# Retention attention and a multiplicative feed-forward: queries loaded four tokens to a partition, in tiles of four heads

## The chip, the core and the metric

The kernel runs on one core of a Trainium2 chip. Five engines work side by side on their own instruction queues: TensorE (PE, matrix products; PEld are its weight loads), VectorE (DVE), ScalarE (ACT), GpSimd (POOL) and SyncE (SP), whose queue here does nothing but issue DMA transfers. Sixteen DMA engines carry the transfers. The metric is the device time of the whole kernel in microseconds (us), smaller is better. Before the change it is 183.44 us, the median of three runs (183.2 to 184.47).

## The reference

There are 4 batches, 8 heads, 768 tokens and 64 elements a head. For each batch and head a 64 x 64 state runs through the tokens, and its output feeds a feed-forward network with three products:

```
gamma = 1.0 - 2.0 ** (-5.0 - np.arange(H))
state = gamma * state + outer(k[t], v[t])        # per batch and head
y[t]  = q[t] @ state / sqrt(64)
x = y.transpose(0, 2, 1, 3).reshape(3072, 512)   # tokens x (heads x 64)
out = ((x @ w1) * (x @ w2)) @ w3 @ w_out         # d_ff = 1024
```

Inputs and output are float32.

## The kernel before

**Tiling.** The recurrence is done in chunks: within a chunk of 128 tokens (two halves of 64) as masked products, between chunks through a state. A step m handles one chunk of two batches: steps 0 to 5 are the six chunks of batches 0 and 1, steps 6 to 11 those of batches 2 and 3. Only steps 0 and 1 are different: `Pairs` (L397) takes 256 tokens of one batch each. The products W3 x W_out are formed once at the start (`w3_transpose`, `w3_part`, `W3Block`), so that the feed-forward of a step is: `ab(f)` for eight blocks f (two products of 128 x 256, a copy by ScalarE, a multiplication by VectorE; L630 to L651), and `o_unit(e)` for two batches (eight products of 128 x 512, a copy, a store; L653).

**Attention of a step.** Four groups of 32 small matmuls (64 x 64 quarters of the array): `scores` (L375, k against q into `psA`), `intra` (L522, masked scores against v into `psY`), `kv` (L538, k against v into `psK`; 16 matmuls only in steps 5 and 11, the last chunks), and `inter` (L591, the state `t` against q, added to `psY`). `outputs_back` (L607) multiplies `psY` by the decays `YS` and writes the tokens of `XT` in their natural order. `ended` (L585) puts a tiny copy, the mark, on ScalarE after the last matmul of `intra`, and `inter` waits for it.

**Where q comes from.** `load_q(n)` (L71) loads tile n, 256 tokens (two chunks) of one batch and all eight heads, through `load_pairs` (L79): two neighbouring tokens stand on a partition, so that a contiguous run in memory is 2 x 64 floats, 512 bytes. `q_cast` (L280) turns the tile into float16 on GpSimd and puts the token's parity t outside the heads. The tile is then transposed in blocks of 128 columns: by TensorE for n = 0 to 3 (`q_transposes`, L318), by a DMA that transposes for n = 4 to 11 (`q_dma`, L336). After that each partition holds a head's element, with even tokens and odd tokens in two runs. `queries` (L368) picks the 64 columns of a half chunk: 2 runs of 32. The order of the columns, even tokens before odd ones, is known to three other places: the masks (`keep`, `keep_t`, L175), the exponents of the decays (`if_i`, L153) and `outputs_back`. k and v of steps 2 to 11 are loaded token by token (256 bytes a run, L93).

**Order of the work.** Nothing is planned by the compiler; the lines from L688 are the order on every engine. All loads, DMA transposes and most stores go through SyncE's queue in the order of the program. At the beginning this is: weights W3 and W_out, tiles of steps 0 and 1, W1, W2, then q 2, q 3, k 2, v 2, k 3, q 4, q 5, v 3, k 4, v 4. In a step m: the DMA transpose of k of step m + 1, the stores of step m - 2, one q tile, k and v of step m + 2, and in even steps the DMA transposes of two q tiles. `step(m)` (L880) starts with `intra(m - 1)`, `kv(m)`, `scores(m)` and `inter(m - 1)` one behind the other. For the steps in `EARLY` (L876), `intra(m - 1)` is instead issued in the step before, after two of the eight `ab` blocks, and `inter` needs no mark.

```
last = None if m in EARLY else ended(intra(m - 1))
...
inter(m - 1, last)
...
if m + 1 in EARLY:
    intra(m)
```

Of the kernel before, what the change touches and what calls it, by code (L numbers as in the profile page):

```python
# [12 lines left out]
MULT = mybir.AluOpType.mult  # L13
# [5 lines left out]
def kernel(  # L19
# [11 lines left out]
    nc = tc.nc  # L31
    B, H, S, D = q.shape
    C = 128
    L = 64
    WST = 22
    NCH = S // C
# [22 lines left out]
    def half(x):  # L59
        return slice(x * L, (x + 1) * L)  # L60

    def dma_in(dst, src):
        nc.sync.dma_start(dst, src)  # L63
# [5 lines left out]
    q_in, k_in, v_in = {}, {}, {}  # L69

    def load_q(n):  # L71

        g, e = divmod(n, 2)
        if g >= NSTEP // 2:
            return
        bp, cp = divmod(g, NCH // 2)
        q_in[n] = load_pairs(q, bp * 2 + e, cp)

    def load_pairs(src, b, cp):  # L79
        t = new_stage()  # L80
        dma_in(
            t[:, :].rearrange("p (h x) -> p h x", x=2 * D),
            src[b, :, cp * 2 * C : (cp + 1) * 2 * C, :].rearrange("h (p t) d -> p h (t d)", t=2),
        )
        return t
# [19 lines left out]
    def new_stage():  # L105
        return wstage.tile([128, 1024], FP, tag="wst", name="stg")
# [18 lines left out]
    for f in range(4, 8):  # L125
        w3_st.append(load_rows(moe_w3, f))
    for e in range(2):
        load_q(e)
        k_in[e] = load_pairs(k, e, 0)
        v_in[e] = load_pairs(v, e, 0)  # L130
    w1_st = [load_rows(moe_w1, d) for d in range(4)]
# [19 lines left out]
    for s in range(2):  # L151
        nc.gpsimd.iota(ip_i[half(s), 0:2, :], pattern=[[1, 2], [0, H]], base=1, channel_multiplier=2)
    if_i = const.tile([128, 2, L], mybir.dt.int32, name="if_i")  # L153
    nc.gpsimd.iota(if_i[:, :, :], pattern=[[L, 2], [1, 2], [2, 32]], base=1, channel_multiplier=0)
    LGH = const.tile([128, H], FP, name="LGH")
    LGP = const.tile([128, 2, NP], FP, name="LGP")
    for h in range(H):
# [2 lines left out]
    YS = const.tile([128, 3, NP, L], FP, name="YS")  # L160
# [12 lines left out]
    def masks_and_decays():  # L173

        nc.gpsimd.memset(keep[:, :], 1.0)  # L175
        for s in range(2):
            r = slice(s * L, (s + 1) * L)
            nc.gpsimd.affine_select(
                out=keep[r, :], in_=keep[r, :], compare_op=mybir.AluOpType.is_ge, fill=0.0,
                base=0, pattern=[[1, 2], [2, 32]], channel_multiplier=-1,  # L180
            )

        nc.gpsimd.memset(keep_t[:, :, :], 1.0)
        for s in range(2):
            for t in range(2):
                nc.gpsimd.affine_select(
                    out=keep_t[half(s), t, :], in_=keep_t[half(s), t, :], compare_op=mybir.AluOpType.is_ge,
                    fill=0.0, base=-t, pattern=[[1, 2], [2, 64]], channel_multiplier=-2,
                )
        for h in range(H):  # L190
            for s in range(2):
                nc.gpsimd.memset(LGP[half((h + s) % 2), s, h // 2 : h // 2 + 1], math.log(gam[h]))
        for h in range(H):
            p, r = h // 2, (h % 2) * 64
            nc.gpsimd.memset(GS[r : r + 64, p : p + 1], gam[h] ** C)
# [11 lines left out]
    XT = {}  # L207
# [70 lines left out]
    q16s, k16s, v16s, qTs, kTs, AMs, psYs, Ts = {}, {}, {}, {}, {}, {}, {}, {}  # L278

    def q_cast(n, *engs):  # L280
        if n not in q_in:
            return
        q16s[n] = att.tile([128, 1024], HP, tag="q16", name="q16", bufs=2)
        pairs_cast(q16s[n], q_in.pop(n), *engs)

    def pairs_cast(dst, src, *engs):
        n = H // len(engs)
        for i, eng in enumerate(engs):
            hs = slice(i * n, i * n + n)
            (nc.scalar.copy if eng is nc.scalar else eng.tensor_copy)(  # L290
                dst[:, :].rearrange("i (t h d) -> i h t d", t=2, d=D)[:, hs, :, :],
                src[:, :].rearrange("i (h t d) -> i h t d", t=2, d=D)[:, hs, :, :],
            )

    def k_cast(m, engs):
        k16 = att.tile([128, 2, 512], HP, tag="k16", name="k16", bufs=3)
        k32 = k_in.pop(m)
        if len(engs) == 1:
            parts = [(k16[:, :, :].rearrange("p e x -> p (e x)"), k32[:, :, :].rearrange("p e x -> p (e x)"))]
        else:  # L300
            parts = [(k16[:, e, :], k32[:, e, :]) for e in range(2)]
        for eng, (dst, src) in zip(engs, parts):
            (nc.scalar.copy if eng is nc.scalar else eng.tensor_copy)(dst, src)  # L303
        k16s[m] = k16
# [61 lines left out]
        )  # L366

    def queries(m, e, p, s, r):  # L368
        c = m % NCH
        i0 = c % 2 * 64 + s * 32  # L370
        return qTs[m // 2 * 2 + e][half(r), :, p, i0 : i0 + 32]

# [24 lines left out]
    class Pairs:  # L397
# [4 lines left out]

        def k_cast(self, *engs):
            self.k16 = att.tile([128, 1024], HP, tag="k16", name="k16", bufs=3)
            pairs_cast(self.k16, k_in.pop(self.e), *engs)

        def k_transposes(self, tag, on_dve, parts=1):
            self.kT = att.tile([128, 2, NP, 128], HP, tag="kT", name="kT", bufs=2)
# [9 lines left out]
            )  # L418

        def queries(self, r, p, s):  # L420
            return qTs[self.e][half(r), :, p, half(s)]

        def scores(self, t):
            am = att.tile([128, 2, NP, 128], HP, tag="am", name="am")
# [18 lines left out]
        def intra(self, t):  # L443
            if t == 0:
                self.y = [bank(f"Y{s}", [128, NP, 128], FP, "psY") for s in range(2)]
            for p in range(NP):
                for s in range(2):
                    for r in range(2):
                        c0 = p * 128 + r * 64
                        last = nc.tensor.matmul(  # L450
                            self.y[s][half(r), p, :], lhsT=self.v16[half(s), t, c0 : c0 + 64],
                            rhs=self.am[t][half(s), r, p, :], start=(t == 0 and p == 0),
                            stop=(s == 0 and t == 1 and p == NP - 1),
                        )
            return last
# [50 lines left out]
        def outputs_back(self, s):  # L506
            if self.e not in XT:
                XT[self.e] = xpool.tile([128, NP * 2, 2, L], HP, tag="xt", name="xt")
            nc.vector.tensor_tensor(
                XT[self.e][:, :, :, :].rearrange("p (a s) b x -> p a s (b x)", s=2)[:, :, s, :]  # L510
                .rearrange("p a (b i t) -> p a t b i", b=2, t=2),
                self.y[s][:, :, :].rearrange("p a (t b i) -> p a t b i", t=2, b=2),
                YS[:, 0:2, :, :].rearrange("p b a (t i) -> p a t b i", t=2), MULT,
            )


# [68 lines left out]
    def ended(mm, eng=None):  # L585

        mark = (eng.tensor_copy if eng else nc.scalar.copy)(mark_t[:, :], Z[0:1, 0:1])
        wait_for(mark, mm)
        return mark
# [17 lines left out]
    def outputs_back(m, s):  # L607
        if m not in XT:
            XT[m] = xpool.tile([128, NP * 2, 2, L], HP, tag="xt", name="xt")
        swap = s == 1 and m % NCH > 0  # L610
        for to in (half(0), half(1)) if swap else (slice(0, 128),):
            fr = half(1 - to.start // L) if swap else to
            n = fr.stop - fr.start
            nc.vector.tensor_tensor(  # L614
                XT[m][to, :, s, :].rearrange("p (a e) (i t) -> p a e t i", e=2, t=2),
                psYs[m][s][fr, :, :].rearrange("p (a e) (t i) -> p a e t i", e=2, t=2),
                YS[fr, s + swap, :, :].unsqueeze(2).broadcast_to((n, NP, 2, L))
                .rearrange("p a e (t i) -> p a e t i", t=2),
                MULT,
            )  # L620

# [106 lines left out]
    wb.mm(4)  # L728
    wb.back()
    q_cast(0, nc.gpsimd)  # L730
    wb = W3Block(5)
    wb.mm(4)
# [117 lines left out]
    def step2():  # L850
        am_back = scores(2)
        am_back(0)
        am_back(1)
        stores.append(f0.o_unit(1, store=False))
        k_cast(3, (nc.gpsimd, nc.scalar))
        for n in (4, 5):
            q_cast(n, nc.gpsimd)
        for n in (4, 5):
            q_dma(n)
        for store in stores:  # L860
            store()
        for f in range(2, 5):
            f1.ab(f)
        intra(2)
        kv_back = kv(2, True)
        kv_back(0)
        f1.ab(5)
        k_transposes(3, None)
        f1.ab(6)
        kv_back(1)  # L870
        v_cast(3, (nc.gpsimd, nc.gpsimd))
        f1.ab(7)

    EARLY = (6, 11, 12)  # L876

    K_PE = (3, 5)

    def step(m):  # L880

        kv_backs = []
        if m > 4:
            last = None if m in EARLY else ended(intra(m - 1))
            if m < NSTEP:
# [27 lines left out]
        for f in range(2):  # L913
            ffn[m - 1].ab(f)
        if m + 1 in EARLY:
            intra(m)
# [61 lines left out]
```

## Time and profile before

| what | value |
|---|---|
| time, median of 3 | 183.44 us |
| profiled span | 181.5 us |
| TensorE busy | 175.3 us (97%) |
| VectorE, ScalarE, GpSimd busy | 108.6, 71.9, 71.3 us |
| DMA packets | 79,531, of which 57,361 under 512 B |
| DMA moved | 39.71 MB, mean 219 GB/s |
| q loads | 12 of 512 KB, 6.4 us from issue to landing (median) |
| k and v loads of steps 2 to 11 | 40 of 256 KB, 5.6 us |
| DMA transposes of q, of k | 8 and 6, 4.9 and 4.6 us |
| granted TensorE clock | 0.999 |

The page of a profile gives busy times, then the span in 40 slices (a digit is a busy share in tenths), the DMA queues, the chain of work that ended last, the costliest groups, and the DMA issues. A line of a timeline is: start, duration, engine, line of the kernel, operation, what is written <- what is read, shapes, and how often; in square brackets stands how long the engine was idle before, and who ended that. A line of the chain in order of time has start, duration and the work. Reading of a row by stretch: from and to, its length, busy time of each engine with the number of instructions, the granted clock, the share of the DMA engines and GB/s.

### The profile page before, as it was taken

What the parts mean: (1) busy time and instruction counts of PE and PEld (TensorE: products, weight loads), DVE (VectorE), ACT (ScalarE), POOL (GpSimd) and SP (SyncE); (2) the same over time, 40 slices, a digit from 0 to 9 for tenths busy, and PEclk for the clock granted to TensorE, in tenths of its full rate; (3) what the DMA queues carried; (4) which work ended last, traced back from release to release, by engine and by line L of the source; (5) the groups of instructions that cost most, each with busy time, mean ns of one, the idle gap of its engine ahead of it and who ended that gap; (6) DMA issues with size and microseconds to landing.
All of it is one profiled execution on the core that took longest, in us unless ns stands there. A gap on an engine that the chain in (4) does not pass through costs nothing.

```text
span 181.5 us, 6220 instructions
## 1 busy us (share of the span) xinstructions
PE 175.3 (97%) x2634; PEld 125.4 (69%) x2634; DVE 108.6 (60%) x204; ACT 71.9 (40%) x156; POOL 71.3 (39%) x127
## 2 busy tenths in 40 slices
PE   7889999999999999999999999999999999999992
PEld 2445656688766785876967858768688587685871
DVE  1246658751769669558477584494674956745430
ACT  3354845555631341524334424244243332442431
POOL 3127536964537752725427273055460350000000
PEclk9999999999999999999999999999999999999999
DMA  5999999999999999999999999999999940201203
GB/s 204 376 417 401 298 291 350 409 371 242 194 256 226 182 301 211 203 312 198 245 202 198 295 169 244 190 208 265 236 114 261 178 149 4 116 0 42 78 0 116
DMA packets 79531, 39.71 MB, mean 219 GB/s; under 512 B 57361, under 2 KB 74001, under 8 KB 79505
## 3 DMA queue, kind: packets, MB, share of 16 engines
q1 hardware_dynamic: 79072, 38.81, 88.6%
q8 instruction: 20, 0.33, 0.8%
q10 hardware_dynamic: 432, 0.52, 0.8%
q14 instruction: 7, 0.05, 0.1%
HBM read 29.36 MB, written 6.29 MB: 196 GB/s over the span
## 4 chain that ended last, share of the span: by engine, by line
PE 88%; DMA 5%; ACT 2%; SPq 1%; DVE 1%; issue 0%; ACTq 0%
PE psF L636 41%; PE psO L663 23%; DMA stg<-in_moe_w_out_dram 5%; PE psF L795 4%; PE psW L269 3%; PE psW L255 3%; PE psY L531 2%; PE psY L599 2%; PE psA L383 2%; PE psG L636 2%; PE psK L551 2%; PE psTq L328 1%; PE psW L244 1%; SPq L63 1%; PE psTk L357 1%; PE psY L450 1%
## 5 line engine op out<-in xcount | busy, mean ns | idle before, releaser
L636 PE MATMUL psF<-xt,w 128*128 128x256 f16 x672 | 76.7, 273 | 0.0
L636 PEld LDWEIGHTS <-w 128*128 128x128 f16 x704 | 68.4, 98 | 10.3
L651 DVE TENSOR_TENSOR ht<-pa,psF 128x256 f16<-128x256 f32 x88 | 36.9, 420 | 37.6 <-PE psF L636 32.0
L645 ACT COPY pa<-psF 128x256 f32<-128x256 f32 x80 | 29.8, 373 | 37.5 <-PE psF L636 37.5
L663 PE MATMUL psO<-w3o,ht 128*128 128x512 f16 (+2 forms) x200 | 43.9, 371 | 0.0
L667 ACT ACTIVATE osb<-psO 128x512 f32<-128x512 f32 (+2 forms) x25 | 14.5, 581 | 44.0 <-PE psO L663 44.0
L663 PEld LDWEIGHTS <-ht 128*128 128x128 f16 x200 | 18.5, 98 | 19.4
L614 DVE TENSOR_TENSOR xt<-psY,YS 64x512 f16<-64x512 f32 (+1 forms) x29 | 21.1, 727 | 4.8 <-PE psY L599 4.4
L310 POOL TENSOR_TENSOR v<-stg,VS 128x512 f16<-128x512 f32 x20 | 20.6, 1042 | 5.4 <-DMA stg<-in_v_dram 5.4
L303 POOL CAST k<-stg 128x512 f16<-128x512 f32 x18 | 11.0, 612 | 26.1 <-DMA stg<-in_k_dram 25.9
L290 POOL CAST q<-stg 128x1024 f16<-128x1024 f32 (+1 forms) x12 | 12.0, 1003 | 17.9 <-DMA stg<-in_q_dram 13.8
L390 DVE TENSOR_TENSOR am<-psA,keep 128x512 f16<-128x512 f32 x20 | 12.8, 682 | 0.6 <-PE psA L383 0.6
L566 POOL TENSOR_TENSOR t<-s,GS 128x512 f16<-128x512 f32 x8 | 8.3, 1039 | 7.8 <-DVE s L565 7.8
L248 DVE COPY w3t<-psW 128x1024 f16<-128x1024 f16 x8 | 5.5, 690 | 5.3 <-PE psW L244 5.3
L269 PE MATMUL psW<-wo,w3t 128*128 128x512 f16 x32 | 8.6, 381 | 0.0
L255 PE MATMUL psW<-wo,w3t 128*128 128x512 f16 x32 | 8.0, 387 | 0.7 <-ACT wo L224 0.5
L795 PE MATMUL psF<-xt,w 128*128 128x256 f16 x64 | 8.3, 273 | 0.2
L686 PE MATMUL psZ<-zeros 128*128 128x512 f16 (+1 forms) x18 | 6.6, 504 | 1.3 <-DVE zeros L143 1.3
L795 PEld LDWEIGHTS <-w 128*128 128x128 f16 x64 | 5.8, 98 | 1.8 <-ACT w L769 0.6
L573 DVE TENSOR_TENSOR t<-psK,t 128x512 f16<-128x512 f32 x9 | 6.2, 690 | 0.6 <-PE psK L551 0.5
L244 PEld LDWEIGHTS <-w3h 128*128 128x128 f16 x64 | 4.4, 103 | 3.1 <-DVE w3h L231 1.7
L225 POOL CAST wo<-stg 128x512 f16<-128x512 f32 x4 | 2.5, 613 | 10.2 <-DMA stg<-in_moe_w_out_dram 10.2
(92 smaller groups left out, 149.3 us busy)
## 6 DMA issues: line engine op xcount, KB each, us to landing
stg<-in_moe_w_dram SPq DMA_DIRECT2D x16, 512.0 KB, 8.8
stg<-in_q_dram SPq DMA_DIRECT2D x12, 512.0 KB, 6.4
out_dram<-osb SPq DMA_DIRECT2D x22, 256.0 KB, 3.3
stg<-in_k_dram SPq DMA_DIRECT2D x20, 256.0 KB, 5.6
stg<-in_v_dram SPq DMA_DIRECT2D x20, 256.0 KB, 5.6
stg<-in_moe_w_out_dram SPq DMA_DIRECT2D x4, 512.0 KB, 7.9
stg<-in_k_dram SPq DMA_DIRECT2D x2, 512.0 KB, 9.5
stg<-in_v_dram SPq DMA_DIRECT2D x2, 512.0 KB, 8.6
```

The costliest lines, as they stand in the source:

```text
L255: nc.tensor.matmul(acc[f], lhsT=w3t[f][:, g * 128 : (g + 1) * 128], rhs=WO[i][:, r, :], start=(g == 0), stop=(g == 7),)
L269: nc.tensor.matmul(self.ps[:, :], lhsT=self.t[:, g * 128 : (g + 1) * 128], rhs=WO[g // 2][:, g % 2, :], start=(g == 0), stop=(g == 7),)
L290: (nc.scalar.copy if eng is nc.scalar else eng.tensor_copy)(dst[:, :].rearrange("i (t h d) -> i h t d", t=2, d=D)[:, hs, :, :], src[:, :]. ...
L310: eng.tensor_tensor(v16[:, e, :].rearrange("j (h d) -> j h d", d=D), v32[:, e, :].rearrange("j (h d) -> j h d", d=D), VS[:, 2, :].unsqueez ...
L390: nc.vector.tensor_tensor(am[:, r, :, :], ps[r][:, :, :], keep[:, :].unsqueeze(1).broadcast_to((128, NP * 2, L)), MULT,)
L614: nc.vector.tensor_tensor(XT[m][to, :, s, :].rearrange("p (a e) (i t) -> p a e t i", e=2, t=2), psYs[m][s][fr, :, :].rearrange("p (a e) (t ...
L636: nc.tensor.matmul(ps[:, :], lhsT=W[d][:, f * 128 : (f + 1) * 128], rhs=self.x(d), start=(d == 0), stop=(d == 3),)
L645: nc.scalar.copy(self.pa[f][:, :], ps[:, :])
L651: nc.vector.tensor_tensor(self.HT[:, f, :], self.pa.pop(f)[:, :], ps[:, :], MULT)
L663: nc.tensor.matmul(psO[:, :], lhsT=self.HT[:, f, e * 128 : (e + 1) * 128], rhs=W3O[f][:, cs], start=(f == 0), stop=(f == 7),)
L667: nc.scalar.activation(osb[:, cs], psO[:, :], AF.Copy, scale=final_scale)
L795: nc.tensor.matmul(ps[f // 2][:, f % 2, :], lhsT=W[d][:, f * 128 : (f + 1) * 128], rhs=f0.x(d), start=(d == 0 and f % 2 == 0), stop=(d == ...
```

## The change

Queries of steps 2 to 11 (counted from one: 3 to 12) come in other tiles. Tile n is now one half of the heads (four) of both batches of the step, in place of all heads of one batch. Batch e stands on partitions 64 e to 64 e + 63, and each partition has four neighbouring tokens, so that a contiguous run is 4 x 64 floats, 1,024 bytes. A tile is loaded by two transfers of 64 partitions each, in place of one of 128. The tile's size, the cast, the transposes and their number stay.

All that knows the order of tokens follows: `queries` picks 4 runs of 16 columns from the tile of the head pair's half; masks, exponents and `outputs_back` have four groups of tokens (t = 4) in place of two; steps 0 and 1, whose queries are still loaded in pairs, read them with a stride of two elements, so that their tokens come in the same order of four groups. `pairs_cast` becomes `token_cast` with the number of tokens as an argument.

Apart from this, step 11 leaves `EARLY`: its `intra(10)`, `kv(11)`, `scores(11)` and `inter(10)` stand in one group, with the mark in between. The aim is fewer and longer runs for the query loads, and one change less between large and small matmuls.

```diff
     def load_q(n):
-        g, e = divmod(n, 2)
+        g, hh = divmod(n, 2)
...
-        q_in[n] = load_pairs(q, bp * 2 + e, cp)
+        q_in[n] = new_stage()
+        for e in range(2):
+            dma_in(
+                q_in[n][half(e), :].rearrange("p (h x) -> p h x", h=4),
+                q[bp * 2 + e, hh * 4 : hh * 4 + 4, cp * 2 * C : (cp + 1) * 2 * C, :]
+                .rearrange("h (p t) d -> p h (t d)", t=4),
+            )
...
-        load_q(e)
+        q_in[e] = load_pairs(q, e, 0)
...
-    nc.gpsimd.iota(if_i[:, :, :], pattern=[[L, 2], [1, 2], [2, 32]], base=1, channel_multiplier=0)
+    nc.gpsimd.iota(if_i[:, :, :], pattern=[[L, 2], [1, 4], [4, 16]], base=1, channel_multiplier=0)
...
-        pairs_cast(q16s[n], q_in.pop(n), *engs)
+        token_cast(q16s[n], q_in.pop(n), 2 if n < 2 else 4, *engs)
...
     def queries(m, e, p, s, r):
-        c = m % NCH
-        i0 = c % 2 * 64 + s * 32
-        return qTs[m // 2 * 2 + e][half(r), :, p, i0 : i0 + 32]
+        qT = qTs[m // 2 * 2 + p // 2][half(r), :, :, :].rearrange("p t a i -> p (t a) i")
+        i0 = e * 64 + m % NCH % 2 * 32 + s * 16
+        return qT[:, p % 2 : 8 : 2, i0 : i0 + 16]
...
         def queries(self, r, p, s):
-            return qTs[self.e][half(r), :, p, half(s)]
+            return qTs[self.e][half(r), :, p, half(s)].rearrange("d t (i u) -> d u t i", u=2)
...
-                XT[m][to, :, s, :].rearrange("p (a e) (i t) -> p a e t i", e=2, t=2),
-                psYs[m][s][fr, :, :].rearrange("p (a e) (t i) -> p a e t i", e=2, t=2),
+                XT[m][to, :, s, :].rearrange("p (a e) (i t) -> p a e t i", e=2, t=4),
+                psYs[m][s][fr, :, :].rearrange("p (a e) (t i) -> p a e t i", e=2, t=4),
...
-    EARLY = (6, 11, 12)
+    EARLY = (6, 12)
```

More of the change, by code (lines that the diff above doesn't have):

```diff
@@ L179, in masks_and_decays @@
                 out=keep[r, :], in_=keep[r, :], compare_op=mybir.AluOpType.is_ge, fill=0.0,
-                base=0, pattern=[[1, 2], [2, 32]], channel_multiplier=-1,
+                base=0, pattern=[[1, 4], [4, 16]], channel_multiplier=-1,
             )
@@ L187, in masks_and_decays @@
                     out=keep_t[half(s), t, :], in_=keep_t[half(s), t, :], compare_op=mybir.AluOpType.is_ge,
-                    fill=0.0, base=-t, pattern=[[1, 2], [2, 64]], channel_multiplier=-2,
+                    fill=0.0, base=-t, pattern=[[1, 4], [4, 32]], channel_multiplier=-2,
                 )
@@ L283, in q_cast, with token_cast @@
         q16s[n] = att.tile([128, 1024], HP, tag="q16", name="q16", bufs=2)
-        pairs_cast(q16s[n], q_in.pop(n), *engs)
-    def pairs_cast(dst, src, *engs):
-        n = H // len(engs)
+        token_cast(q16s[n], q_in.pop(n), 2 if n < 2 else 4, *engs)
+    def token_cast(dst, src, t, *engs):
+        n = 1024 // D // t // len(engs)
         for i, eng in enumerate(engs):
@@ L290, in pairs_cast @@
             (nc.scalar.copy if eng is nc.scalar else eng.tensor_copy)(
-                dst[:, :].rearrange("i (t h d) -> i h t d", t=2, d=D)[:, hs, :, :],
-                src[:, :].rearrange("i (h t d) -> i h t d", t=2, d=D)[:, hs, :, :],
+                dst[:, :].rearrange("i (t h d) -> i h t d", t=t, d=D)[:, hs, :, :],
+                src[:, :].rearrange("i (h t d) -> i h t d", t=t, d=D)[:, hs, :, :],
             )
@@ L404, in k_cast @@
             self.k16 = att.tile([128, 1024], HP, tag="k16", name="k16", bufs=3)
-            pairs_cast(self.k16, k_in.pop(self.e), *engs)
+            token_cast(self.k16, k_in.pop(self.e), 2, *engs)
         def k_transposes(self, tag, on_dve, parts=1):
@@ L510, in outputs_back @@
                 XT[self.e][:, :, :, :].rearrange("p (a s) b x -> p a s (b x)", s=2)[:, :, s, :]
-                .rearrange("p a (b i t) -> p a t b i", b=2, t=2),
-                self.y[s][:, :, :].rearrange("p a (t b i) -> p a t b i", t=2, b=2),
-                YS[:, 0:2, :, :].rearrange("p b a (t i) -> p a t b i", t=2), MULT,
+                .rearrange("p a (b i t) -> p a t b i", b=2, t=4),
+                self.y[s][:, :, :].rearrange("p a (t b i) -> p a t b i", t=4, b=2),
+                YS[:, 0:2, :, :].rearrange("p b a (t i) -> p a t b i", t=4), MULT,
             )
@@ L614, in outputs_back @@
             nc.vector.tensor_tensor(
-                XT[m][to, :, s, :].rearrange("p (a e) (i t) -> p a e t i", e=2, t=2),
-                psYs[m][s][fr, :, :].rearrange("p (a e) (t i) -> p a e t i", e=2, t=2),
+                XT[m][to, :, s, :].rearrange("p (a e) (i t) -> p a e t i", e=2, t=4),
+                psYs[m][s][fr, :, :].rearrange("p (a e) (t i) -> p a e t i", e=2, t=4),
                 YS[fr, s + swap, :, :].unsqueeze(2).broadcast_to((n, NP, 2, L))
-                .rearrange("p a e (t i) -> p a e t i", t=2),
+                .rearrange("p a e (t i) -> p a e t i", t=4),
                 MULT,
```

## The prediction, made before the change was run

> **What bounds the kernel now.** I read the page first: its busy times, its forty slices and its chain.
>
> ```profile
> span 181.5 us, 6220 instructions
> ...
> PE 175.3 (97%) x2634; PEld 125.4 (69%) x2634; DVE 108.6 (60%) x204; ACT 71.9 (40%) x156; POOL 71.3 (39%) x127
> ...
> DMA  5999999999999999999999999999999940201203
> ...
> PE 88%; DMA 5%; ACT 2%; SPq 1%; DVE 1%; issue 0%; ACTq 0%
> ```
>
> TensorE is busy 97% of the span and carries 88% of the chain, at a granted clock of 0.999. The DMA engines are also full, up to about 146 us. So the change touches two full resources, and only TensorE's time, or a load that comes too late for TensorE, can move the end. Next, the chain in order of time: from 42.92 us to the last output TensorE's pieces join end to end, but for one gap of 0.10 us at 116.71. No query load is waited for there. Three places matter: the start of step 2, step 5, and step 11.
>
> ```profile
> 45.71 0.45 PE psTq L328 x8
> ...
> 47.03 0.45 PE psTq L328 x8
> ...
> 48.34 0.45 PE psTk L357 x8
> ...
> 72.68 6.99 PE psF L636 x64
> 79.67 0.38 PE psY L531 x32
> ...
> 80.86 3.56 PE psO L663 x16
> ...
> 144.37 1.75 PE psF L636 x16
> 146.12 0.37 PE psY L531 x32
> 146.49 5.35 PE psF L636 x48
> ...
> 152.74 3.56 PE psO L663 x16
> ```
>
> The first three rows are the transposes of q tiles 2 and 3 and of k of step 2. How near their loads are to being late stands in the timelines of GpSimd and ScalarE:
>
> ```profile
> 43.35 1.04 POOL L290 CAST q<-stg 128x1024 f16<-128x1024 f32 x1 [1.24 <-DMA stg<-in_q_dram]
> 45.18 1.04 POOL L290 CAST q<-stg 128x1024 f16<-128x1024 f32 x1 [0.79 <-DMA stg<-in_q_dram]
> ...
> 47.21 0.62 ACT L303 CAST k<-stg 128x512 f16<-128x512 f32 x1
> ```
>
> Both q casts start when the DMA lands, 1.83 us apart. The second ends at 46.22, 0.81 us before its transposes (47.03); the k cast ends at 47.83, 0.51 us before its own (48.34). The second half of k was issued at 41.38 and landed 5.81 us later, at 47.19, so it too is set by the DMA. Last, rates by stretch, in GB/s at the end of each row:
>
> ```profile
> 8.00:16.00 8.00, 7.10 (x50) 3.78 (x50) 3.64 (x7) 3.72 (x6) 2.58 (x7) 1.00 1.02 414
> 20.00:28.00 8.00, 7.79 (x87) 4.47 (x88) 4.96 (x10) 4.96 (x9) 3.79 (x6) 1.00 1.16 291
> 44.00:48.00 4.00, 4.00 (x44) 3.38 (x43) 3.14 (x6) 2.55 (x5) 1.99 (x3) 1.00 0.99 203
> ```
>
> The first stretch moves weight rows (4,096 B runs), the second token pairs (512 B), the third single k and v tokens (256 B): the run's length sets the rate.
>
> **What the Trainium skill says.** "SBUF — State Buffer", Door 1: The DMA port swizzle: partitions 0 to 63 reach only 8 of the 16 write ports, as do 64 to 127; it gives 196 GB/s measured and 218 GB/s as the limit for 64 partitions. The same page, "Can I just issue two DMAs to hit both halves?": two such transfers gained only 6% over one. The trace of before can't confirm either, as its big loads all write 128 partitions. The same Door 1 section on cachelines: 16-bit elements may be read with strides up to 8 elements inside a 16-byte line without loss; here only a strided weight load is seen (103 ns at L244 against 98 ns), no strided moving operand. "TensorEngine Tiling (Array Packing)", Key Properties: a change of tiling mode drains TensorE; step 11 against step 5 below agrees, with 0.19 us.
>
> **The change part by part.**
>
> Query loads, ten tiles of 512 KB (n = 2 to 11). Removed: one transfer of 1,024 runs of 512 B over 128 partitions. Added: two transfers of 256 runs of 1,024 B over 64 partitions each. Price per run on one of 16 engines, from the rates: 4,096 B at 414/16 GB/s is 158 ns, 512 B at 291/16 is 28.1 ns; the line through both is 9.6 ns + 0.0362 ns per byte (it gives 18.9 ns for 256 B, 217 GB/s, against the 203 seen). So a tile takes 64 x 28.1 = 1.80 us before, which the 1.83 us between the casts supports. After, there are two bounds. If nothing but the engines limits it: 1,024 B is 46.7 ns, 32 x 46.7 = 1.49 us, 0.31 less. If the ports limit it: 512 KB at 218 GB/s is 2.40 us (an estimate from the Door 1 section), 0.60 more; at 196 it is 2.67, 0.87 more. I take the ports at 218: the fixed part of a single transfer is overlapped here by the full queue, and eight ports cannot take the 352 GB/s that 1.49 us would need.
>
> What that does at step 2, with 0.60 per tile: q 2's cast starts at 43.95 and ends at 44.99, still ahead of 45.71. q 3 lands 1.20 later: cast 46.38 to 47.42, so its transposes slip from 47.03 to about 47.45. k's second half lands at 48.39; ScalarE casts it until 49.01, and the k transposes slip from 48.34 to about 49.05. That contains the first slip: 0.7 us in all. Behind the k cast in ScalarE's queue stands the copy of q 3's transposes (1.01 us), then done at 50.04, ahead of the slipped scores (49.65 + 0.7). The queue behind TensorE's wait is the rest of the kernel, so the 0.7 is paid in full.
>
> Later steps. q 4 and q 5 land 1.8 and 2.4 later. q 5's cast would end near 59.9, then a state decay (1.04) and v's casts (2.04) near 62.9, against intra of step 3 at 61.68 + 0.7 = 62.4: up to 0.6 more, less what the DMA's idle tenth around 48 to 52 us gives back. I take 0, because only the second half of v is late and the first 16 of 32 matmuls don't read it; 0.6 goes into the range. Beyond, the queue catches up with TensorE every second step: its stores go out at 97.47 and 121.56, 0.62 and 0.84 after the psO pieces end (96.85, 120.72), the time that the output copy takes. So +1.2 per two steps doesn't pile up, and the transposes of q land 2.9 to 4.7 us ahead of the scores at steps 4 to 10 (65.95 against 68.80, 111.52 against 116.27).
>
> Ten more DMA issues: an unblocked one takes 0.4 us on the SyncE queue. They lie in the five microseconds between issue and landing: nothing.
>
> Casts and DMA transposes: the same count and sizes (1.04 us a cast); the destination's runs stay 64 elements. Nothing.
>
> Moving operands. scores and inter of steps 2 to 11 read 4 runs of 16 in place of 2 runs of 32, the same bytes and lines: nothing. The first two steps' queries are read with a stride of two elements: 64 matmuls of L429 (16 in 0.40 us) and 16 of L498 (8 in 0.39). Between nothing and twice as long, 4 x 0.40 + 2 x 0.39 = 2.4 us. I take nothing, by the cacheline sentence.
>
> VectorE's output copies write with a stride of 4 elements instead of 2 (727 ns each at L614). Between nothing and a third more, three of them are 0.7 us, and 1.1 us lies between the third's end (143.08) and the matmuls that read it (144.21): hidden at either end. Masks and index tables: the same sizes, nothing.
>
> Step 11 loses its early intra. Step 5 has the same work in one group: from 72.68 to 80.86, 8.18 us. Step 11, in two: 144.37 to 152.74, 8.37 us. So -0.19 us. The added wait is the mark on ScalarE, behind which only the output copy stands (0.60 us, needed 1.8 us later). In step 5 the mark starts at 80.16 and takes 0.20, and inter starts at 80.41 without a gap; same here.
>
> Sum: +0.7 - 0.2 = +0.5, and 183.44 + 0.5 = **184.0**.
>
> **The rivals.** (1) The ports don't bind: each tile is 0.31 us faster, TensorE waits for no load anyway, and only the -0.19 stays: 183.2. For it: k loads follow q in the same queue and may fill the idle ports; against: both halves of a tile go through all engines one after the other. This one ends faster than before. (2) The ports bind harder (0.87 a tile): k's second half is 1.74 late, 1.2 us at step 2, 0.6 at step 3, and about 0.3 at step 5, whose k transpose lands at 78.12 for 80.22: 183.44 + 2.1 - 0.2 = 185.3. (3) The strided moving operand costs double: 183.44 + 2.4 - 0.2 = 185.6 (186.1 with the port stall). For it, nothing in the trace; against, the cachelines. (4) A gain beyond 1% would need 1.8 us of TensorE's time, and the edits remove 0.2: nearly excluded.
>
> **How the numbers follow.** Forecast 0.45, rival 1 0.34, rival 2 0.13, rival 3 0.06, rival 4 0.02. Rivals 2 and 3 lie at or over +1% (185.3), most of them beyond with the spread of the times: slower 0.16; faster 0.02; same 0.82. The range leaves out rival 4 and the larger half of 2 and 3: 182.9 to 185.3.
>
> **What would show it.** In the profile after: 5,120 fewer packets, 74,411. The two q casts near 43 us start 2.4 us apart (1.5 if rival 1 holds, 2.7 if rival 2). A wait of TensorE at psTq or psTk of step 2, 0.7 us together, which the chain shows as a DMA or cast piece (none in rival 1). Step 11 from its first psF to its psO in 8.2 us. L429 at 0.40 us for 16 (0.8 in rival 3). The forecast fails if writes of 64 partitions run at full rate, or if the early loads have more room than the casts' ends show.

## The result, and the profile after

The changed kernel takes 195.82 us (median of 6 runs, 193.65 to 198.18), against 183.57 us for the kernel before on the same chip (6 runs, 183.2 to 184.47). Single runs of any kernel can fall into a slower state, so while the medians given here are of all runs, the ratios and the losses in us compare the means of the other runs alone. The ratio is 1.0636, with a 95% interval of 1.0572 to 1.07, a loss of 11.7 us. The forecast of 184.0 us was 11.8 us too low, and the time lies far above the range's upper end of 185.3 us. No rival had it either.

The page of the changed kernel, with the rows that answer to those shown of before:

```profile
span 194.5 us, 6236 instructions
...
PE 178.2 (92%) x2634; PEld 123.8 (64%) x2634; DVE 125.8 (65%) x204; ACT 72.8 (37%) x157; POOL 71.5 (37%) x127
...
DMA packets 74570, 39.71 MB, mean 204 GB/s; under 512 B 57520, under 2 KB 69040, under 8 KB 74544
...
PE 42%; DMA 23%; DVE 19%; SPq 10%; issue 2%; POOL 1%; ACT 1%; ACTq 0%; DVEq 0%; POOLq 0%
```

TensorE's share of the chain fell from 88% to 42%. DMA went from 5% to 23%, and VectorE from 1% to 19%. VectorE's busy time rose by 17.2 us with the same 204 instructions, so its instructions became longer. One group holds nearly all of that. Its row in the page of before, and then in that of after:

```profile
L614 DVE TENSOR_TENSOR xt<-psY,YS 64x512 f16<-64x512 f32 (+1 forms) x29 | 21.1, 727 | 4.8 <-PE psY L599 4.4
```

```profile
L620 DVE TENSOR_TENSOR xt<-psY,YS 64x512 f16<-64x512 f32 (+1 forms) x29 | 37.3, 1292 | 5.5 <-PE psY L605 5.3
```

These are the output copies. One takes 1.29 us where it took 0.73 us, with the same shapes and types. The answer on what TensorE waited for, from 44 us to the end (columns: total us, times, longest), shows who suffers. psF are the first products of the feed-forward, psO its output products, psTq the transposes of q, psA the scores:

```profile
PE psF L642 <- DVE xt L620: 3.3, 7, 0.5
PE psTq L334 <- POOL q L296: 1.6, 2, 0.9
PE psO L669 <- issue: 1.0, 1, 1.0
PE psA L389 <- DMA kT<-k: 0.9, 1, 0.9
PE psF L642 <- DVE t L579: 0.6, 1, 0.6
PE psF L642 <- DVE s L571: 0.2, 1, 0.2
```

The list counts idle time alone. Products overlap (one of psF starts every 0.11 us and lasts 0.27), so a tile that comes late loses more than is listed here.

**Where the time went.** The first output product of each step (psO) starts in the two traces at these times (us), with the delay that each step adds. The last row is the last output products, after the twelve steps:

| Step | Before | After | Added | What stands in the trace after |
|---|---|---|---|---|
| 2 | 47.32 | 50.68 | 3.36 | q tile 3 lands at 48.98 |
| 3 | 56.30 | 59.67 | 0.01 | |
| 4 | 69.05 | 73.61 | 1.19 | one gap of TensorE, 1.03 |
| 5, 6, 7 | 105.01 | 112.05 | 2.48 | psF waits for xt |
| 8 | 117.09 | 124.82 | 0.69 | wait for a DMA transpose, 0.85 |
| 9, 10, 11 | 152.67 | 164.41 | 4.01 | psF waits for xt |
| 12 and tails | 177.34 | 190.40 | 1.32 | psF waits for xt |

The rows that wait for the output copies sum to 7.8 us of 13.06. The start of step 2 is 3.4, and steps 4 and 8 add 1.9.

**One step, read closely.** First VectorE of before in step 10, between 140 and 145 us (start, duration, line, work), then TensorE at the same place:

```profile
140.87 2.21 DVE L614 TENSOR_TENSOR xt<-psY,YS 128x512 f16<-128x512 f32 x3 [0.78 <-PE psY L599]
143.11 0.69 DVE L573 TENSOR_TENSOR t<-psK,t 128x512 f16<-128x512 f32 x1
143.83 0.69 DVE L565 TENSOR_TENSOR s<-psK,t 128x512 f32<-128x512 f32 x1
```

```profile
140.74 3.63 PE L663 MATMUL psO<-w3o,ht 128*128 128x512 f16 x16
144.21 1.91 PE L636 MATMUL psF<-xt,w 128*128 128x256 f16 x16
```

Step 10 of the changed kernel, again VectorE and then TensorE:

```profile
151.41 3.90 DVE L620 TENSOR_TENSOR xt<-psY,YS 128x512 f16<-128x512 f32 x3 [0.78 <-PE psY L605]
155.34 0.69 DVE L579 TENSOR_TENSOR t<-psK,t 128x512 f16<-128x512 f32 x1
156.06 0.69 DVE L571 TENSOR_TENSOR s<-psK,t 128x512 f32<-128x512 f32 x1
```

```profile
151.28 3.63 PE L669 MATMUL psO<-w3o,ht 128*128 128x512 f16 x16
155.36 4.87 PE L642 MATMUL psF<-xt,w 128*128 128x256 f16 x36 [0.46 <-DVE xt L620]
```

While TensorE works off sixteen output products, VectorE has five things to do: three output copies, then two updates of the state that read psK. The matmuls that follow (psF, four to a tile) read the copies' result, and psF and psK share one pool of four PSUM banks. So the first psF tile waits for the third copy, and the next two wait each for a bank that a state update has read. Single instructions show it. In after the three tiles start at 155.36, 156.09 and 156.81, each 0.05 to 0.06 us after the end of a VectorE instruction (155.31, 156.03, 156.75). In before they start at 144.21, 144.64 and 145.08, the pace of TensorE itself, while VectorE had ended at 143.08, 143.80 and 144.52. The slack was therefore 1.13, 0.84 and 0.56 us. Three copies that are 0.57 us longer each cost 1.70 us and eat all three. The third tile is 1.19 us later after the first output product than before. Step 9, in which the two kernels do the same work in the same order, is 13.23 us long in place of 11.80.

### The profile page after: what moved, and what is told of

It is laid out like the page before. It is cut to its first block, busy times and chain, and to the rows that moved or that the text cites. A ratio compares the mean times of both kernels' runs of the same rounds, so it can differ in the third digit from the quotient of the medians.

```text
span 194.5 us, 6236 instructions
## 1 busy us (share of the span) xinstructions
PE 178.2 (92%) x2634; PEld 123.8 (64%) x2634; DVE 125.8 (65%) x204; ACT 72.8 (37%) x157; POOL 71.5 (37%) x127
## 2 busy tenths in 40 slices
DMA packets 74570, 39.71 MB, mean 204 GB/s; under 512 B 57520, under 2 KB 69040, under 8 KB 74544
## 4 chain that ended last, share of the span: by engine, by line
PE 42%; DMA 23%; DVE 19%; SPq 10%; issue 2%; POOL 1%; ACT 1%; ACTq 0%; DVEq 0%; POOLq 0%
PE psF L642 30%; DVE xt L620 15%; SPq L63 10%; DMA stg<-in_q_dram 6%; PE psO L669 5%; DMA stg<-in_v_dram 5%; DMA stg<-in_moe_w_dram 5%; DMA stg<-in_moe_w_out_dram 5%; DMA kT<-k 3%; PE psY L537 2%; DVE t L579 1%; DVE s L571 1%; PE psA L389 1%; PE psY L605 1%; PE psK L557 1%
## 5 line engine op out<-in xcount | busy, mean ns | idle before, releaser
L642 PE MATMUL psF<-xt,w 128*128 128x256 f16 x672 | 78.3, 273 | 4.8 <-DVE xt L620 3.3
L642 PEld LDWEIGHTS <-w 128*128 128x128 f16 x704 | 67.4, 98 | 19.4 <-DVE xt L620 4.8
L657 DVE TENSOR_TENSOR ht<-pa,psF 128x256 f16<-128x256 f32 x88 | 36.4, 420 | 31.9 <-PE psF L642 31.1
L620 DVE TENSOR_TENSOR xt<-psY,YS 64x512 f16<-64x512 f32 (+1 forms) x29 | 37.3, 1292 | 5.5 <-PE psY L605 5.3
L801 PE MATMUL psF<-xt,w 128*128 128x256 f16 x64 | 8.4, 273 | 0.6 <-DVE xt L515 0.5
L801 PEld LDWEIGHTS <-w 128*128 128x128 f16 x64 | 5.8, 98 | 2.6 <-ACT w L775 0.5
L231 POOL CAST wo<-stg 128x512 f16<-128x512 f32 x4 | 2.4, 612 | 10.3 <-DMA stg<-in_moe_w_out_dram 10.3
```

The costliest lines, as they stand in the source:

```text
L620: nc.vector.tensor_tensor(XT[m][to, :, s, :].rearrange("p (a e) (i t) -> p a e t i", e=2, t=4), psYs[m][s][fr, :, :].rearrange("p (a e) (t ...
L642: nc.tensor.matmul(ps[:, :], lhsT=W[d][:, f * 128 : (f + 1) * 128], rhs=self.x(d), start=(d == 0), stop=(d == 3),)
L657: nc.vector.tensor_tensor(self.HT[:, f, :], self.pa.pop(f)[:, :], ps[:, :], MULT)
L801: nc.tensor.matmul(ps[f // 2][:, f % 2, :], lhsT=W[d][:, f * 128 : (f + 1) * 128], rhs=f0.x(d), start=(d == 0 and f % 2 == 0), stop=(d == ...
```

## The experiments

The theory after the result, called V in the expectations: the output copies' stride sets the time, and the transfers are a smaller part. Its rival, called P, was that the transfers set it. Two later questions follow: what of a strided copy costs, and why half transfers delay so much. Ratios are against the kernel before, on the same chip.

### The changed kernel with dense output copies

```diff
-                XT[m][to, :, s, :].rearrange("p (a e) (i t) -> p a e t i", e=2, t=4),
+                XT[m][to, :, s, :].rearrange("p (a e) (t i) -> p a e t i", e=2, t=4),
```

> The changed kernel, with the output copies of the steps written in the order in which they are read, so that neighbouring elements stand side by side (the tokens of a half chunk then stay in four groups, and the rows of the output with them); the loads stay as changed. Theory V (VectorE's copies, 1293 ns instead of 727, hold back the feed-forward): the copies fall to 727 ns or less and the time falls by the 9.8 us that were added after the start of step 2, to about 186. Theory P (the transfers into 64 partitions are the cause, through late k, v and q): the copies get faster as well, but the time stays over 192.

Measured: 188.99 us, ratio 1.0319 (1.024 to 1.0399), a loss of 5.4 us. The edit is in the 29 copies of L620; the four of the first two steps keep their stride. The copies' row of this kernel's page:

```profile
L620 DVE TENSOR_TENSOR xt<-psY,YS 64x512 f16<-64x512 f32 (+1 forms) x29 | 20.0, 689 | 5.5 <-PE psY L605 5.2
```

One pattern of addresses, changed on the write side alone, brings a copy from 1,292 to 689 ns and wins back 6.3 of the 11.7 us. Theory P, over 192 us, falls; theory V had the direction, but 9.8 us as the size. The waits of psF for xt are gone. What stays over before in this trace is mostly loads and gaps: 1.57 us at the start of step 2, 0.9 at step 4 and 2.2 at step 10.

### The kernel before with copies of stride 4

In both output copies (L511 to L513 of the first two steps, L615 to L618 of the others):

```diff
-                XT[m][to, :, s, :].rearrange("p (a e) (i t) -> p a e t i", e=2, t=2),
-                psYs[m][s][fr, :, :].rearrange("p (a e) (t i) -> p a e t i", e=2, t=2),
+                XT[m][to, :, s, :].rearrange("p (a e) (i t) -> p a e t i", e=2, t=4),
+                psYs[m][s][fr, :, :].rearrange("p (a e) (t i) -> p a e t i", e=2, t=4),
...
```

> The kernel before, with nothing changed but the output copies, which write with a stride of four elements as in the changed kernel (so tokens land in other columns and output rows). Theory V: the copies take 1293 ns, and the time rises to about 192. Theory P: the copies may slow down, but they are hidden behind the 3.6 us of the output products; the time stays within 1 us of before, at most 184.5.

Measured: 193.53 us, ratio 1.0569 (1.052 to 1.0618), a loss of 10.3 us. The copies' row:

```profile
L614 DVE TENSOR_TENSOR xt<-psY,YS 64x512 f16<-64x512 f32 (+1 forms) x29 | 37.3, 1293 | 4.8 <-PE psY L599 4.5
```

Theory P, at most 184.5 us, falls. The stride alone, without one changed load, loses nearly as much as the whole change (11.7). Step 2 starts 2.08 us late here too, with its queries loaded as before. In the chain before it stand the copies of the first two steps (L509, 1.32 us), which didn't before.

### The changed kernel with each query tile in one transfer

```diff
-        q_in[n] = new_stage()
-        for e in range(2):
-            dma_in(
-                q_in[n][half(e), :].rearrange("p (h x) -> p h x", h=4),
...
+        q_in[n] = load_pairs(q, bp * 2 + hh, cp)
```

> The changed kernel, with each query tile loaded by one transfer of 128 partitions in runs of 512 bytes as before (the same bytes in all; the tile's contents then stand in another order than the later code takes them for, so the output is another); copies and groups as changed. Theory V: only the late start of step 2 (3.2 us) is won back, 192 to 193. Theory P: the time falls to 184 to 186.

Measured: 193.7 us, ratio 1.0575 (1.0529 to 1.0622), a loss of 10.4 us. Only 1.3 us come back. It agrees with the experiment before it (10.3), which has the same copies and the same loads. What this kernel has beyond that one (the order in which queries are read, the masks, step 11) costs nothing that can be told.

### The kernel before with half transfers

The opposite: only queries of steps 2 to 11 come as two transfers of 64 partitions, as in the change.

```diff
-        q_in[n] = load_pairs(q, bp * 2 + e, cp)
+        if n < 2:
+            q_in[n] = load_pairs(q, bp * 2 + e, cp)
+            return
+        hh = e
+        q_in[n] = new_stage()
+        for e in range(2):
+            dma_in(
+                q_in[n][half(e), :].rearrange("p (h x) -> p h x", h=4),
...
```

> The kernel before, with nothing changed but the query loads of steps 2 to 11, which are the two transfers of 64 partitions and runs of 1,024 bytes of the changed kernel (contents in another order than the later code takes them for, so the output is another). Theory V: step 2 starts 3.2 us late, later steps lose little: 186 to 187. Theory P: about 194.

Measured: 189.88 us, ratio 1.0342 (1.0264 to 1.042), a loss of 6.2 us and more than theory V gave. TensorE's waits after 44 us in this trace:

```profile
PE psA L393 <- DMA kT<-k: 1.8, 1, 1.8
PE psTq L338 <- POOL q L300: 1.7, 2, 0.9
PE psF L646 <- issue: 1.4, 1, 1.4
...
PE psO L673 <- issue: 0.6, 1, 0.6
```

So the transfers have a cost of their own, and not at the start alone: step 2 starts 3.74 us late, a DMA transpose of k at step 8 is waited for, and there are two gaps in which the profile shows nothing waited for. Copies alone (10.3) and transfers alone (6.2) sum to 16.5 us, but together they lose 11.7. At least half of the overlap lies in the start of step 2: 2.08 and 3.74 us late apart, 3.36 together. The two kernels that are equal to the changed one up to there (the one with dense copies above, and the one with step 11 in two groups below) start it 1.57 and 2.23 us late, so a single trace is uncertain here by up to 2 us. Late loads and late copies may pass at the same time, which no run takes apart.

### Step 11 in one group, alone and undone

```diff
-    EARLY = (6, 11, 12)
+    EARLY = (6, 12)
```

In the kernel before:

> The kernel before, with step 11 in one group and nothing else changed. From the chain: step 11 from 8.37 to 8.18 us, so 0.19 less in all; the ratio 0.999, which the interval will hardly tell from 1. If the mark on ScalarE is waited for, 0.1 to 0.3 us more instead.

Measured: 183.92 us (22 runs) against 184.31 (27 runs), ratio 0.9991 (0.9966 to 1.0017). Step 11 in the chain of this kernel, in order of time:

```profile
145.17 6.99 PE psF L636 x64
...
153.35 3.56 PE psO L663 x16
```

From 145.17 to 153.35 are 8.18 us, against 8.37 in before: the forecast's 0.19. In the whole time 0.19 us is too little to be told from nothing, even with 22 runs.

The opposite, the changed kernel with step 11 in two groups (`EARLY = (6, 11, 12)`):

> The changed kernel, but with step 11 among the steps whose intra is issued early, as before. All theories: the group alone is worth 0.2 us in the kernel before, 0.19 by the chain; here VectorE's copies bound the steps, so that the time stays within 0.5 us of the changed kernel's, 195.5 to 196.3.

Measured: 195.01 us, ratio 1.0576 (1.0511 to 1.064), a loss of 10.9 us: just below the range expected, with an interval that overlaps that of the changed kernel. The loss is there without this edit, and a share of the edit can't be told from nothing.

### What of a strided copy costs

A kernel with no matrix work measures copies of 512 elements a partition by themselves: float32 from PSUM times float32 from SBUF into float16, with the strides on either side; one-source copies on three engines; and float32 results.

> No part of the reference is computed (the output is zeros): VectorE multiplies the same 512 elements a partition, float32 from PSUM times float32 from SBUF, four times for each way of writing the result. Theory S (the stride of the float16 write is the cost): stride 1 about 690 ns, stride 2 about 727, stride 4 and 8 about 1290, whether in runs of 16 or 32 elements; a float32 result slows at stride 2 (8 bytes) as well. Theory R (the runs of 16 in place of 32 are the cost): runs of 32 at stride 4 take 727, runs of 16 at stride 2 and 1 take 1290. Dense writes with strided reads from PSUM: 690 if only the write matters, 1290 if any stride does. Copies of ScalarE and GpSimd at strides 2 and 4 show whether it is VectorE's own.

Measured, ns for one (median of four), by the stride of the write in elements:

| Written | 1 | 2 | 4 | 8 |
|---|---|---|---|---|
| float16, VectorE, two sources | 691 | 722 | 1285 | 2400 |
| float32, VectorE, two sources | | 692 | 1058 | |
| float16, VectorE, one source | | 720 | 1279 | |
| float16, ScalarE, one source | | 723 | 1280 | |
| float16, GpSimd, one source | | 752 | 1310 | |

Rows of its page, of 128x512 each, with means (in order: stride 4 in runs of 32, where one of the four took 1,502 ns; stride 2 in runs of 16; dense writes with the source read at strides of 16 or 32 elements):

```profile
L50 DVE TENSOR_TENSOR s4r<-ps,Y 128x512 f16<-128x512 f32 x4 | 5.4, 1344 | 0.1
L50 DVE TENSOR_TENSOR s2r<-ps,Y 128x512 f16<-128x512 f32 x4 | 2.9, 730 | 0.1
L50 DVE TENSOR_TENSOR r<-ps,Y 128x512 f16<-128x512 f32 x8 | 5.4, 688 | 0.2
```

A stride of 2 is nearly free, 4 costs 1.86 times as much as dense and 8 costs 3.5 times. The length of the runs doesn't matter, nor, at strides 2 and 4, does the engine (no dense copy of ScalarE or GpSimd was measured), and strided reads from PSUM cost nothing. It is the write to SBUF. Theory R falls. Theory S holds up to stride 4 and misses twice: stride 8 isn't like 4, and float32 at stride 2 isn't slow.

### The stride moved to the read side

If that is so, the copies can write densely and read psY with a stride instead. In all 33 copies of the changed kernel (the index table `if_i` follows):

```diff
-                XT[m][to, :, s, :].rearrange("p (a e) (i t) -> p a e t i", e=2, t=4),
-                psYs[m][s][fr, :, :].rearrange("p (a e) (t i) -> p a e t i", e=2, t=4),
+                XT[m][to, :, s, :].rearrange("p (a e) (i t) -> p a e i t", e=2, t=4),
+                psYs[m][s][fr, :, :].rearrange("p (a e) (t i) -> p a e i t", e=2, t=4),
...
```

> The changed kernel, with the output copies turned round: they read PSUM with a stride of 16 elements and write XT without gaps, all 33 of them, the decays kept in the order of the tokens; the loads stay as changed, and the result is the reference's. Theory V with the strides measured alone (dense writes 691 ns whatever the read): the copies take about 690 ns and the time falls to that of the changed kernel with ungapped writes, 187 to 189; what is left over before is the two transfers. If reads are slow in this place, copies near 1290 and 194 to 196.

Measured: 190.35 us, ratio 1.0278 (1.020 to 1.0356), a loss of 5.1 us, with copies of 688 ns. It wins back 6.6 us, and no wait for xt is left; the rival, slow reads and 194 to 196 us, falls. The 5.1 us that stay agree, within the intervals, with the 6.2 that the half transfers lose alone.

The same in the kernel before (t = 2, and step 11 in one group):

> The kernel before, with the same turn of the output copies (stride 32 reads, ungapped writes) and with step 11 in one group; the loads as before. The copies fall from 727 to about 690 ns, two of them near the path of the start (0.1 us), and step 11 gives 0.19 us: 0.2 to 0.3 us less, a ratio of about 0.9985, hardly to be told from 1.

Measured: 183.81 us (22 runs) against 184.04 (27 runs), ratio 0.9986 (0.9958 to 1.0014). Copies of 688 in place of 727 ns buy nothing that can be told, as they had slack. No kernel tried beats the one before.

### What half transfers cost by themselves

A kernel without computation loads six tiles of 512 KB in four ways.

> No part of the reference is computed (the output is zeros): six query tiles of 512 KB are loaded, in four ways one after the other, each beginning when the one before has landed. Token pairs on 128 partitions: 1.8 us a tile. Two transfers of 64 partitions from one queue: theory Q (eight of sixteen ports) 2.4 us a tile; rival (the engines alone) 1.5. Runs of 1,024 bytes on 128 partitions: 1.5 in both. The two halves issued from two queues at once (SyncE and ScalarE): 1.5 to 1.8 if packets of the two alternate and so fill both sets of ports, 2.4 if they don't.

| Way | us a tile | GB/s |
|---|---|---|
| pairs, 512 B runs, 128 partitions | 1.80 | 291 |
| two halves of 64 partitions, 1,024 B runs, one queue | 2.28 | 230 |
| 1,024 B runs, 128 partitions | 1.51 | 347 |
| two halves, issued by SyncE and ScalarE at once | 1.92 | 273 |

The figures are from one execution; the last row lies between its two forecasts. The half transfer is bound by the partitions it reaches: the same runs on 128 partitions go at 347 GB/s. That a half is also the smaller transfer isn't the reason, as the list of DMA packets in this trace shows: a packet of 1,024 bytes takes 48 ns (median) in the third way and 76 in the second. The Trainium skill ("SBUF — State Buffer", Door 1) gives 218 GB/s as the limit for 64 partitions. The 230 measured here, for two such transfers behind each other, lie above it, so the measurement decides; as an estimate the page's figure served. A tile costs 0.48 us more, and two tiles 1.0. But step 2 lost 3.4.

A second kernel puts six tiles of weight rows ahead of two tiles of queries, as they stand at the start of the kernel before. The theory under test, called O in the expectation, is that half transfers delay the transfers ahead of them:

> No part of the reference is computed (the output is zeros): twice over, six weight loads (512 KB, 128 partitions), then two query tiles, then one k tile in two halves; the query tiles first as one transfer each, then as two of 64 partitions. Theory O (engines that are ahead begin the 64-partition transfers while others still write weights to the same ports): the last weight loads land 1 us or more later than the 1.28 us apart of the first way, and from the last weight to the last query more than 4.6 us pass or the two add up to it. Theory N (strict order): the weights land as in the first way, and the four halves follow 1.15 us apart.

Measured: from the landing of the fifth weight tile to that of the last query 4.99 us with whole transfers, and 7.68 with halves. That is 2.7 us more, not 1.0. Of this, 1.28 us lies in the last weight tile, whose transfer is the same in both ways: it lands 1.33 us after the one before it in the first way, and 2.61 in the second. Landings alone don't prove it, as the third weight tile of the second way is late too (2.41 us after the second), before any packet of a half transfer.

The packets do. In the changed kernel 43 weight packets of 4,096 bytes start later than 38.86 us, half a microsecond after the first 1,024-byte packet of a query; they take 314 ns (median). At the same place of before, where the query packets have 512 bytes, 35 of them start, and they take 162. The other kernels agree: 269 to 368 ns in the four that have half transfers at this place, 159 to 162 in the five that haven't. So packets of a half transfer run beside those of the transfer ahead of it and slow them, as theory O has it. That they meet at the same ports is its explanation, and no run shows that part.

### Half transfers from step 4 on

The kernel before, with `if n < 4:` in the edit above, so that step 2 and all that precedes it keep their loads.

> The kernel before, with the two transfers of 64 partitions only for the query tiles of steps 4 to 11 (contents in another order than the later code takes them for, so the output is another); those of steps 2 and 3 as before. If the late start of step 2 is the main harm of the transfers: step 2's first output product is back at 47.3 us and the time within 1 us of before, 183.6 to 184.6. If the later tiles harm by themselves, late k and v in steps 5 to 10: 185 to 187.

Measured: 188.24 us, ratio 1.022 (1.0152 to 1.0287). Step 2 starts at 47.23, as before (47.32): the start's loss is gone. But a loss of 4.0 us stays, and the time lies above both forecasts. What TensorE waited for:

```profile
PE psO L673 <- issue: 2.1, 1, 2.1
PE psA L393 <- DMA kT<-k: 1.4, 1, 1.4
PE psF L646 <- issue: 0.5, 1, 0.5
```

So the later half transfers harm by themselves, by late k and by gaps without a visible releaser. Both occur with whole transfers too, but are rarer: the kernel with step 11 in one group has one such gap of 0.67 us, and the kernel before with turned copies waits 1.0 us for kT.

**The gaps.** The chain of this kernel in order of time, around the largest:

```profile
56.28 2.91 PE psO L673 x13
59.19 2.07 issue
61.26 0.81 PE psO L673 x3
```

TensorE stops in the middle of a row of equal products, and the profile shows no input that is missing. In the list of DMA packets one of 16,384 bytes of the queue that carries instructions runs from 58.42 to 59.70, and TensorE goes on 1.55 us after its end. The other gaps are like that: in the changed kernel it ends at 62.13 and the gap at 63.68; with dense copies at 137.22 and 138.73; in the kernel before with half transfers at 139.66 and 141.26. In before the packet for the place of 59.19 ends at 56.62, and if TensorE needs the same 1.5 us, that is 58.1 us, before it gets there. Over the traces of all eleven full kernels, TensorE has eleven gaps of over 0.15 us after 44 us that the profile puts down to nothing. Each ends 1.50 to 1.61 us after such a packet, and ten of them are in kernels with half transfers. So late instructions behind a crowded DMA are the likely cause. It is an association, and no experiment took it apart.

## Why the prediction was wrong

**The output copies: the step that failed.** The prediction said: "VectorE's output copies write with a stride of 4 elements instead of 2 (727 ns each at L614). Between nothing and a third more, three of them are 0.7 us, and 1.1 us lies between the third's end (143.08) and the matmuls that read it (144.21): hidden at either end." Three things are wrong in it.

- The size. A copy takes 78% more (1,292 ns), so three of them are 1.70 us, not 0.7. The upper bound of a third stood on no row and no price. The Trainium skill ("SBUF — State Buffer", Door 1, on cachelines) lets 16-bit elements stride by 8 within a 16-byte line without loss. For float16 writes the runs contradict that: 1,285 ns at stride 4 and 2,400 at stride 8, against 691.
- The slack. The 1.1 us is that of the first psF tile. Behind the copies stand two state updates in VectorE's queue, and their reads free the banks for the second and third tile. The third tile had 0.56 us, so even the prediction's own 0.7 would have shown.
- The number of places. The cost recurs in nearly every step, so a wrong "hidden" is multiplied: 7.8 us in the trace, 10.3 when the copies are changed alone.

**The ports.** Half right. The transfers do bind, at 230 GB/s for the forecast's 218: the q casts start at 46.91 and 49.13, 2.22 us apart, and a tile alone takes 2.28 where 2.40 was forecast. Rival 1 (no bind) and rival 2 (196 GB/s) both fall by that measurement. But step 2 starts 3.36 us late, not 0.7 (1.57 to 3.74 in the five kernels that have the half transfers there). The chain of the changed kernel shows the path that the prediction named:

```profile
36.69 12.30 DMA stg<-in_q_dram
...
49.13 1.05 POOL q L296
...
50.23 0.62 PE psTq L334 x8
```

The term that was mis-sized is the landing of the second q tile: "q 3 lands 1.20 later", and it is 3.95 (48.98 for 45.03); in the other four of these traces 2.2 to 4.3. Of the 3.95, 3.47 are there already when the last weights ahead of it land (44.91 for 41.44); between that weight and q only 0.48 is added. Some 0.84 of the 3.47 are older than the first packet of a half transfer (a weight tile lands at 37.95 for 37.11), and why is open. The prediction priced the half transfer by itself, and left the transfers ahead of it alone.

**Later steps.** "+1.2 per two steps doesn't pile up" holds in that no delay grows from step to step. "I take 0" does not hold: without any change at step 2, the later half transfers cost 4.0 us. "Ten more DMA issues … nothing" stays open. In the chain after, four issues of 0.6 us each (two of q, where before has one, and two of k) stand one behind the other ahead of the v load (108.46) that leads to the late kT at step 8, but no run separates issues from transfers.

**The moving operands.** Right: the 64 matmuls of L435 have a median of 214 ns, against 216 at L429 before, with a stride of two elements. Rival 3 falls; here what the Trainium skill says of cachelines ("SBUF — State Buffer", Door 1) holds, for a read at a stride of 2. (The 186.1 given for rival 3 with the port stall takes step 11's 0.2 off twice; it should be 186.3.)

**Step 11.** Right in the kernel before: 8.18 us, as worked out, and too small to matter. In the changed kernel itself the same stretch takes 9.05 us (155.36 to 164.41), as the copies' waits lie in it. Packets: 74,570, with 74,411 forecast.

**The range.** 82% stood on "same", because the only costs thought to reach the end were loads. The one item with no row behind it was bounded by a guess and then called hidden, so its true size lay outside every rival.

## What to carry to other kernels

A change of layout moves a stride somewhere: look for it on the write side of 16-bit results, where four elements apart costs nearly double here, and put it on the read of PSUM instead, where it was free. Before a cost is called hidden, add up all that stands in that engine's queue until the next thing that TensorE needs, data and PSUM banks alike; here five instructions of 3.6 us stood against 3.56 us of products, and no slack but 0.56 us was left. A transfer to half the partitions is dear beyond its own bytes when the queue is full, as it delays those under way too.

## What the runs showed of the hardware

- The cost of a strided write is the same on VectorE, ScalarE and GpSimd (1,279, 1,280 and 1,310 ns at stride 4), and it doesn't go by bytes alone: float32 at 2 elements (8 bytes apart) is free with 692 ns, float16 at 4 elements (also 8 bytes) takes 1,285.
- Two half transfers from two queues at once reach 273 GB/s, against 230 from one queue.
- A half transfer slows those ahead of it: weight packets of 4,096 bytes that start beside it take 269 to 368 ns (medians of five traces), and 159 to 162 beside whole query transfers (six traces).
- A packet of 1,024 bytes takes 76 ns in transfers to 64 partitions, and 48 in transfers to 128.
- TensorE can stop for 0.5 to 2.1 us with no input missing that the profile shows. In all eleven such gaps, a 16,384-byte packet of the instruction queue had ended 1.5 to 1.6 us before it went on.
